# Five copies of half stacks for each head: from engine operations to transfers inside SBUF

## The chip, the core and the metric

The kernel runs on one core of a Trainium2 chip. The metric is the time of one execution on the device, in microseconds; the median of three runs is given. The core has a matrix engine (TensorE, PE in the profile, with its weight loads as PEld), a vector engine (VectorE, DVE), an activation engine (ScalarE, ACT), a general engine (GpSimd, POOL) and SyncE (SP), which here does nothing but issue transfers to 16 DMA engines. Each of the five works through its own list of instructions strictly in order; an instruction waits at the head of its list until what it needs is there.

## The reference

Attention with a mask from hashes, and a two-layer network behind it. q, k and v have 4 batches, 8 heads, 768 positions and 64 features. The six signs of q times `proj` make a bucket number for each position, those of k likewise; a query sees only the keys of its own bucket.

```python
mask = q_bucket[:, :, :, None] == k_bucket[:, :, None, :]
scores = scale * np.matmul(q, k.transpose(0, 1, 3, 2))
scores = np.where(mask, scores, -1000000000.0)
scores = scores - np.max(scores, axis=-1, keepdims=True)
attn = np.exp(scores)
attn = attn / (np.sum(attn, axis=-1, keepdims=True) + 1e-09)
attn_out = np.matmul(attn, v).astype(np.float32)
x = attn_out.transpose(0, 2, 1, 3).reshape(B * S, H * D)   # 3072 tokens, 512 features
h = np.maximum(x @ w_in, 0.0)                               # 512 to 2048
out = (h * h @ w_out).astype(np.float32)                    # 2048 to 512
```

## The kernel before

**Recording and planning.** No instruction is issued where it is written. A recording layer collects every operation with its rank (`pr.rank`), its reads and its writes; some operations are recorded with several ways, the same work as an instruction of one engine or of another. A planner then goes over the recorded list with a price for each instruction (`Program.cost`: a duration for the engine's instructions; for a transfer an issue time and its bytes over a rate), chooses a way for each operation and an order for each engine, and does that in four rounds of passes forward and backward. The result is five lists, which are issued. So a price of one kind of transfer enters the place of every operation of the kernel. Nearly all instructions carry the line of the issuing call (L402; groups of matmuls L399), and tiles tell them apart. Where the plan has TensorE idle ahead of the first `pm`, filler matmuls (`idle`, L395) are put in, in proportion to that idle time.

**The attention.** Work is by pairs of heads. `prep` (L564 to 610) loads a head's R (q transposed in partitions 0 to 63, k transposed in 64 to 127), makes `pd` and `bits` (the hashes), and from them stacks of 128 partitions whose product is q times k plus a term for the buckets. T is partitions 0 to 63 and U is 64 to 127. In batches 1 to 3 (24 heads) numbers are split into a rounded part and a rest for the fast float32r form: A (rounded q and k, on ScalarE), L (the rest, on VectorE), and M (the buckets, on VectorE from `pc`). Then halves are moved between stacks: Q[T] from A[U], Q[U] from L[U], A[U] from A[T], L[U] from M[T], M[T] from Q[T]. So of the five copies two depend on earlier copies directly (M[T] waits for Q[T], A[U] is overwritten only when Q[T] has read it), and L[U] is overwritten only when Q[U] has read it. Each copy moves 64 partitions of 768 float32, 192 KB. A, L, Q and M have two buffers each, one for each head of a pair; a head's stacks are built when the last score matmul of the head two before is done. Batch 0 ("plain") uses float32 matmuls on two stacks and other copies, which stay.

**A unit of scores.** `unit` (L651 to 673) treats 128 queries of one head: four matmuls into `pS` (A by Q, then M by L, in two halves of 384 keys), `nmx` (the row maximum, VectorE), `e` (exponential with row sum, ScalarE), `rv` (reciprocal of the sum), `hl` (probabilities as a float16 part and a float16 rest: ScalarE, then VectorE) and one DMA transpose of hl into aT (384 KB). A head has six units, three for each half of its queries. `av` multiplies aT with the split values VV into `pA` (36 matmuls for a head pair and 384 queries, two side by side in the array), and ScalarE and VectorE make `xx` of it. Four xx feed one pass of `moe`: 16 times 12 matmuls `pm`, the squared and split `g` (ScalarE and VectorE, some on GpSimd), and 9 matmuls `po` for each g. The first pm needs the sixth xx. The weights w_in and w_out come in as float32 `raw` and are split into float16 pairs (`top`, `f`, `win`, `wo`; `sq`, `pt`, `norm` for their scales); that is done ahead of the passes that use them, mostly in the first 150 us.

**What the change touches.** `move` (L429) records a copy with the ways ScalarE, VectorE, GpSimd and, where asked, a transfer; `MV` (L424) allows all four. `send` (L426) records one transfer on SP. The copies are L592 to L594 and L607 to L608, and the planner's price of a transfer is L193.

Of the kernel before, what the change touches and what calls it, by code (L numbers as in the profile page):

```python
# [112 lines left out]
class Program:  # L113
# [59 lines left out]
    @staticmethod  # L173
    def cost(key, name, args, kw):

        size = lambda x: int(np.prod(x.shape[1:]))
        column = {F32: 4 / 2.4, F32R: 0.445}
        if name == "matmuls":

            side = {32: 4, 64: 2}.get(size(args[0][0][1]), 1)  # L180
            t = sum(size(a[2]) * column.get(a[2].dtype, 1 / 2.4) + 7 for a, _ in args) / side
            return t, t
        kinds = [x.rec.kind if isinstance(x, View) else "" for x in args]
        ptr = any(isinstance(x, View) and x.shape[-1] == 1 for x in args[2:3])
        n = max(size(args[0]), size(args[1]) if isinstance(args[1], View) else 0)
        if key == "pe":
            t = max(107, size(args[2]) * column.get(args[2].dtype, 1 / 2.4) + 3)
            return t, t
        if name.startswith("dma"):
            b = int(np.prod(args[0].shape)) * mybir.dt.size(args[0].dtype)  # L190
            inside = name == "dma_start_transpose" or kinds[:2] == ["sb", "sb"]
            busy = 1040 if key == "pool" else (650 if inside else 475) + 50 * (key == "act")
            return busy, b / (292 if name == "dma_start_transpose" else 360)  # L193
        if key == "act":
            t = 93 * (isinstance(kw.get("scale"), View) + isinstance(kw.get("bias"), View)) + (51 if "psum" in kinds[:2] else 93) + n / 1.2 + 93 * ("accum_out" in kw)
        elif key == "pool":
            t = 147 + n * (2.1 if args[0].dtype == F32 or args[0].dtype == F32R else 1.88) if name == "tensor_tensor" else 161 + n / 1.2 + 83 * ptr
        else:
            fast = name in ("tensor_copy", "tensor_scalar") and "psum" not in kinds[:2]
            both = len(args) > 3 and isinstance(args[3], View) and args[3].shape[-1] == 1  # L200
            t = 67 + n / (1.92 if fast else 0.96) + 62 * (ptr and (fast or name == "scalar_tensor_tensor")) + 100 * both
        return t, t
# [212 lines left out]
def lsh_attention_moe(ctx: ExitStack, tc, kq, v, proj2, w_in, w_out, consts, out):  # L415
# [6 lines left out]
    T, U = slice(0, D), slice(D, P)  # L422

    MV = (act, dve, pool, sp)  # L424

    def send(out, x):  # L426
        sp.dma_start(out, x)

    def move(out, x, scale=1.0, engines=(act, dve, pool)):  # L429
        ways = [(q, "tensor_scalar", (out, x, scale, 1.0, ALU.mult, ALU.mult), {}) for q in engines if q not in (act, sp)]  # L430
        if act in engines:
            ways.append((act, "activation", (out, x, AF.Identity if isinstance(scale, View) else AF.Copy), {"scale": scale}))
        if sp in engines:
            ways.append((sp, "dma_start", (out if out.dtype == x.dtype else out.bitcast(x.dtype), x), {}))
        pr.add(*ways)

    def left(out, x, scale, part):
        ways = [(dve, "scalar_tensor_tensor", (out, x, scale, part, ALU.mult, ALU.subtract), {})]
        if not isinstance(scale, View) and scale == 1.0:
            ways.append((pool, "tensor_tensor", (out, x, part, ALU.subtract), {}))  # L440
        pr.add(*ways)

    def sb(shape, dtype, name, bufs=1, tag=None):
        return pr.tile(sbp, "sb", shape, dtype, name, BUFS.get(tag or name, bufs), tag)

    def ps(shape, dtype, name, bufs=1, tag=None):
        return pr.tile(psp, "psum", shape, dtype, name, bufs, tag)
# [111 lines left out]
    f32 = lambda x: x.bitcast(F32)  # L559

    def matmuls(*args, start=True, stop=True):
        pr.add((pe, "matmuls", [(a, {"start": start, "stop": stop}) for a in args], {}))

    def prep(b, hp, plain):  # L564
        r0 = pr.rank
        Rs, Rqs = [], []
        for odd in range(2):
            R = sb([P, S], F32, "Q" if odd else "A") if plain else sb([P, S], F32, "R", 2)
            send(R, kq[b, 2 * hp + odd])
            Rs.append(R)  # L570
            if plain:
                Rq = sb([P, S], F32, "R", 2)[T]
                send(Rq, kq[b, 2 * hp + odd, U])
                Rqs.append(Rq)

        pd = ps([P, 512], F32, "pd", tag="misc")[:, 0:HS]
        matmuls(*[(pd[32 * n : 32 * n + 32], pj, Rs[n // 2][:, n % 2 * HS : (n % 2 + 1) * HS]) for n in range(4)])
        bits = sb([P, HS], BF16, "bits")
        act.activation(bits, pd, AF.Sign, scale=2.0**60, bias=thr)
        out = []  # L580
        for odd, R in enumerate(Rs):
            pr.rank = r0
            if plain:
                M = sb([P, S], F32, "M" if odd else "L")
            else:

                A, L, Q, M = [sb([P, S], F32R, name) for name in "ALQM"]
                move(A, R, cst[:, 2:3])
                left(L, R, cst[:, 2:3], f32(A))
            pr.rank = r0 + STACKS  # L590
            if not plain:
                move(Q[T], f32(A[U]), 1.0, MV)  # L592
                move(Q[U], f32(L[U]), 1.0, MV)
                move(A[U], f32(A[T]), 1.0, MV)  # L594
            for half in range(2):
                w = slice(half * HS, (half + 1) * HS)
                n = 2 * odd + half
                pc = ps([P, 512], F32, "pc", tag="misc")[:, 0:HS]
                pe.matmul(pc, sgn[:, n * P : (n + 1) * P], bits, start=True, stop=True)
                dve.tensor_scalar(M[:, w], pc, cst[:, 0:1], cst[:, 1:2], ALU.subtract, ALU.max)  # L600
            if plain:

                move(R[U], M[T], 1.0, MV)
                move(M[T], Rqs[odd], SC)
                out.append(((M, R),))
            else:
                move(L[U], f32(M[T]), 1.0, MV)  # L607
                move(M[T], f32(Q[T]), 1.0, MV)  # L608
                out.append(((Q, A), (M, L)))
        return out  # L610

# [180 lines left out]
    def ready(b, hp, rank, plain):  # L792

        if (b, hp) not in kept or not alive(x for st in kept[b, hp] for ab in st for x in ab):
            pr.rank = rank
            kept[b, hp] = prep(b, hp, plain)
# [64 lines left out]
```

## Time and profile before

| quantity | value |
|---|---|
| median of 3 runs | 935.48 us (934.19 to 935.99) |
| the profiled execution | 930.39 us |
| its span | 928.3 us |
| TensorE busy | 884.9 us (95%) |
| ScalarE busy | 741.1 us (80%) |
| VectorE busy | 646.0 us (70%) |
| GpSimd busy | 77.4 us (8%) |
| DMA engines, share of the span | 64.4% (main queue) |

A busy share is a mean over stages that differ. Ahead of the first pm TensorE does only scores, pA and filler; in the middle it has scores and pm and po to fill with; at the end pm and po alone. TensorE's ends are modelled, so that a matmul that waits inside the pipeline can be counted as busy; the pitch from one matmul to the next in a stretch without waits tells the work. Waits are put down to the releaser that came last.

### The profile page before, as it was taken

The page shows a single profiled execution, that of the slowest core. Times are in us where ns is not written, and L with a number is a line of the kernel's source. Part 1 is how long each engine was busy: PE and PEld are TensorE (multiplying, and loading weights), DVE is VectorE, ACT ScalarE, POOL GpSimd, SP SyncE. Part 2 cuts the span into 40 slices and gives each one's busy share as a digit, 9 for nine tenths or more (in the row PEclk, how much of TensorE's full clock was granted, in tenths as well). Part 3 has the DMA queues.
Part 4 walks back from the last instruction along what each step waited for, and adds up shares of the span by engine and source line. Part 5 has one row for each costly group of instructions (what it writes and reads, how often), then busy time and mean ns, then how long its engine had stood idle before and what let it go on. Part 6 is the DMA issues. An engine that isn't in the chain of part 4 may idle for free. (4 is left out here: it accounts for less than half of the span.)

```text
span 928.3 us, 14714 instructions
## 1 busy us (share of the span) xinstructions
PE 884.9 (95%) x5334; PEld 480.1 (52%) x5334; DVE 646.0 (70%) x1186; ACT 741.1 (80%) x1269; POOL 77.4 (8%) x140
## 2 busy tenths in 40 slices
PE   7878989999999999799999999999999999999997
PEld 5545555445445555455555555555454555554553
DVE  5998999999898877797877766887767651211111
ACT  5888988998999998999898979997979773533433
POOL 0222233310030000010000000000000000000000
PEclk9999999999999999999999999999999999999999
DMA  7999999947777866796767762974566650300000
GB/s 244 258 252 246 244 221 266 242 102 136 145 170 141 159 132 115 170 199 140 155 120 155 125 118 59 185 161 78 111 113 126 110 96 4 82 1 1 35 1 35
DMA packets 319800, 126.55 MB, mean 136 GB/s; under 512 B 303664, under 2 KB 303792, under 8 KB 319728
## 3 DMA queue, kind: packets, MB, share of 16 engines
q1 hardware_dynamic: 319728, 125.61, 64.4%
q8 instruction: 42, 0.69, 0.3%
q14 instruction: 30, 0.25, 0.1%
HBM read 43.59 MB, written 6.29 MB: 54 GB/s over the span
## 5 line engine op out<-in xcount | busy, mean ns | idle before, releaser
L402 PE MATMUL po<-wo,g 128*128 128x512 f16 x1152 | 332.6, 381 | 1.7 <-ACT o L402 0.9
L402 PE MATMUL pm<-xx,win 128*128 128x384 f16 x1536 | 318.1, 326 | 2.9 <-DVE xx L402 1.7
L402 DVE SCALAR_TENSOR_TENSOR hl<-e,rv,hl 128x768 f16<-128x768 f32 x192 | 195.4, 1020 | 27.0 <-ACT hl L402 25.7
L402 DVE TENSOR_REDUCE nmx<-pS 128x1 f32<-128x768 f32 x192 | 182.8, 952 | 41.4 <-PE pS L402 40.3
L402 PEld LDWEIGHTS <-win 128*128 128x128 f16 x1536 | 145.6, 98 | 119.1 <-issue 21.8
L402 ACT ACTIVATE hl<-e,rv 128x768 f16<-128x768 f32 x187 | 173.6, 930 | 23.6 <-DMA aT<-hl 12.2
L402 ACT ACTIVATE e<-pS,nmx 128x768 f32<-128x768 f32 x192 | 171.0, 891 | 23.6 <-DVE nmx L402 16.3
L402 PEld LDWEIGHTS <-g 128*128 128x128 f16 x1152 | 107.1, 98 | 133.3 <-issue 31.6
L402 DVE SCALAR_TENSOR_TENSOR g<-g,g 128x384 f16<-128x384 f32 x118 | 65.4, 554 | 128.9 <-ACT g L402 128.1
L402 ACT ACTIVATE g<-pm 128x384 f32<-128x384 f32 x127 | 61.5, 484 | 102.0 <-PE pm L402 101.5
L399 PE MATMUL pA<-aT,VV 128*64 128x384 f16 x1152 | 125.9, 333 | 4.1 <-DMA aT<-hl 4.0
L402 ACT ACTIVATE g<-g 128x384 f32<-128x384 f32 (+1 forms) x232 | 120.0, 519 | 4.4 <-PE po L402 0.8
L402 PE MATMUL pS<-A,Q 128*128 128x384 f32 x288 | 92.7, 401 | 6.6 <-ACT e L402 5.7
L399 PEld LDWEIGHTS <-VV 128*64 128x64 f16 x1152 | 58.3, 109 | 68.8 <-issue 48.7
L402 POOL TENSOR_SCALAR rv<-sm 128x1 f32<-128x1 f32 x89 | 33.5, 376 | 564.9 <-ACT e L402 563.9
L402 PE MATMUL pS<-L,M 128*128 128x384 f32 x288 | 77.7, 348 | 0.6 <-ACT M L402 0.6
L402 PEld LDWEIGHTS pS<-A,Q 128*128 128x128 f32 x288 | 46.2, 188 | 45.2 <-ACT e L402 38.4
L402 PEld LDWEIGHTS pS<-L,M 128*128 128x128 f32 x288 | 52.4, 188 | 1.4 <-ACT M L402 0.8
L395 PEld LDWEIGHTS <-ones 128*128 128x128 bf16 x498 | 34.4, 106 | 18.1 <-issue 12.5
L402 PE MATMUL pS<-A,L 128*128 128x384 f32 x96 | 36.6, 504 | 6.9 <-ACT e L402 4.7
L402 PE MATMUL pS<-Q,M 128*128 128x384 f32 x96 | 37.9, 511 | 5.0 <-ACT e L402 3.3
L402 DVE TENSOR_SCALAR M<-pc,cst 128x384 fp32r<-128x384 f32 (+1 forms) x56 | 37.5, 670 | 3.8 <-PE pc L402 3.8
(96 smaller groups left out, 695.8 us busy)
## 6 DMA issues: line engine op xcount, KB each, us to landing
RV<-vp SPq DMA_DIRECT2D x32, 384.0 KB
R<-kq SPq DMA_DIRECT2D x24, 384.0 KB
raw<-w_in SPq DMA_DIRECT2D x16, 511.8 KB
raw<-w_out SPq DMA_DIRECT2D x16, 511.8 KB
out<-o SPq DMA_DIRECT2D x21, 256.0 KB
aT<-hl SPq DMA_TRANSPOSE x192
A<-kq SPq DMA_DIRECT2D x4, 384.0 KB
Q<-kq SPq DMA_DIRECT2D x4, 384.0 KB
```

The source lines that it names most:

```text
L395: issue(q, q.engine.matmul(self.idle[0].real(), self.idle[1].real(), self.idle[1].real(), start=True, stop=True).ins)
L399: ins = q.engine.matmul(*map(real, args), **kw).ins
L402: ins = getattr(q.engine, o.name)(*map(real, o.args), **{k: real(x) for k, x in o.kw.items()}).ins
```

## The change

The five copies of a head in batches 1 to 3 are recorded as transfers on SP alone, no longer as a choice. The planner's rate for a transfer goes from 360 to 314 bytes for each ns, that for a transpose from 292 to 175.

```diff
-            return busy, b / (292 if name == "dma_start_transpose" else 360)
+            return busy, b / (175 if name == "dma_start_transpose" else 314)
...
             if not plain:
-                move(Q[T], f32(A[U]), 1.0, MV)
-                move(Q[U], f32(L[U]), 1.0, MV)
-                move(A[U], f32(A[T]), 1.0, MV)
+                send(f32(Q[T]), f32(A[U]))
+                send(f32(Q[U]), f32(L[U]))
+                send(f32(A[U]), f32(A[T]))
...
             else:
-                move(L[U], f32(M[T]), 1.0, MV)
-                move(M[T], f32(Q[T]), 1.0, MV)
+                send(f32(L[U]), f32(M[T]))
+                send(f32(M[T]), f32(Q[T]))
```

Of the 120 copies the planner had put 117 on ScalarE, 2 on VectorE and 1 on SP; now 120 are on SP. The whole order is made anew. Counts that differ: filler matmuls 498 before and 756 now; `top` on VectorE 3 and 19, on GpSimd 29 and 13; `rv` on GpSimd 89 and 74; runs of pA after the first pm 140 and 115. TensorE's other instructions are the same set in another order.

ScalarE in the middle of the kernel, around the preparation of one head (A<-R begins it; g belongs to moe, e and hl to units). Before:

```order
L402 ACTIVATE A<-R,cst 128x768
L402 ACTIVATE g_5586<-pm 128x384
L402 ACTIVATE Q<-A 64x768
L402 ACTIVATE e,sm<-pS,nmx 128x768
L402 ACTIVATE g_5586<-g_5586 128x384
L402 ACTIVATE Q<-L 64x768
L402 ACTIVATE hl<-e,rv 128x768
L402 ACTIVATE A<-A 64x768
L402 ACTIVATE e,sm<-pS,nmx 128x768
L402 ACTIVATE L<-M 64x768
L402 ACTIVATE hl<-e,rv 128x768
L402 ACTIVATE M<-Q 64x768
```

And in the changed kernel, around a head at a like place:

```order
L402 ACTIVATE A<-R,cst 128x768
L402 ACTIVATE hl<-e,rv 128x768
L402 ACTIVATE e,sm<-pS,nmx 128x768
L402 ACTIVATE g_6387<-pm 128x384
L402 ACTIVATE hl<-e,rv 128x768
L402 ACTIVATE g_6387<-g_6387 128x384
L402 ACTIVATE g<-g_6387 128x384
L402 ACTIVATE e,sm<-pS,nmx 128x768
L402 ACTIVATE hl<-e,rv 128x768
L402 ACTIVATE g_6446<-pm 128x384
```

The five copies between A<-R and the next head's work are gone from ScalarE; e, hl and g close up.

SP's list, the only one of transfers. Before, where the one copy stands that was a transfer (RV and R are loads, aT the transposes):

```order
L402 DMA_TRANSPOSE aT<-hl 128x12x128
L402 DMA RV<-vp 128x768
L402 DMA_TRANSPOSE aT<-hl 128x12x128
L402 DMA A<-A 64x768
L402 DMA R<-kq 128x768
L402 DMA_TRANSPOSE aT<-hl 128x12x128 x5
```

And in the changed kernel, around one head in the middle:

```order
L402 DMA Q<-A 64x768
L402 DMA Q<-L 64x768
L402 DMA R<-kq 128x768
L402 DMA_TRANSPOSE aT<-hl 128x12x128
L402 DMA L<-M 64x768
L402 DMA A<-A 64x768
L402 DMA_TRANSPOSE aT<-hl 128x12x128
L402 DMA M<-Q 64x768
```

Five transfers of each head now stand between the transposes, in the order in which SP issues them.

VectorE just ahead of the sixth xx, which releases the first pm. Before, where 236 operations stand ahead of that xx:

```order
L402 RECIPROCAL rv<-rv 128x1
L402 SCALAR_TENSOR_TENSOR win<-f,towin,win 128x512
L402 TENSOR_SCALAR fromwo<-norm 128x1
L402 RECIPROCAL rv<-rv 128x1
L402 TENSOR_REDUCE rows<-RV 128x12
L402 SCALAR_TENSOR_TENSOR f<-raw,top_77 128x512
L402 SCALAR_TENSOR_TENSOR xx<-pA,xx 128x384
```

And in the changed kernel, where 291 stand ahead of it:

```order
L402 SCALAR_TENSOR_TENSOR win<-f,towin,win 128x512 x2
L402 TENSOR_REDUCE nmx<-pS 128x1
L402 SCALAR_TENSOR_TENSOR hl<-e,rv,hl 128x768
L402 SCALAR_TENSOR_TENSOR f<-raw,top_73 128x512
L402 TENSOR_SCALAR top_77<-raw 128x512
L402 RECIPROCAL rv<-rv 128x1
L402 SCALAR_TENSOR_TENSOR xx<-pA,xx 128x384
```

The weights' splitting (top, f, win, wo) and a few units of scores moved ahead of it: 14 more top, 4 more each of f, win and wo, 3 more each of hl and nmx, 10 more rv, 7 more back and some smaller ones. On TensorE 6 more float32 score operations of batch 0 and 7 more pt stand ahead of the first pm.

## Rows read from the trace of the kernel before

**Rows 1.** The page: its span, and each engine's busy time and share.

```profile
span 928.3 us, 14714 instructions
PE 884.9 (95%) x5334; PEld 480.1 (52%) x5334; DVE 646.0 (70%) x1186; ACT 741.1 (80%) x1269; POOL 77.4 (8%) x140
```

**Rows 2.** The chain, pieces without a wait: start us, us, engine, tile, line, count.

```profile
918.68 4.11 PE po L402 x19
...
905.27 1.14 PE pm L402 x7
...
490.40 2.07 PE pA L399 x24
...
489.09 0.70 PE pS L402 x4
```

**Rows 3.** Groups of TensorE's instructions: count, busy us, mean ns, idle before.

```profile
L402 PE MATMUL po<-wo,g 128*128 128x512 f16 x1152 | 332.6, 381 | 1.7 <-ACT o L402 0.9 <-ACT wo L402 0.7
L402 PE MATMUL pm<-xx,win 128*128 128x384 f16 x1536 | 318.1, 326 | 2.9 <-DVE xx L402 1.7 <-ACT g L402 1.0
L399 PE MATMUL pA<-aT,VV 128*64 128x384 f16 x1152 | 125.9, 333 | 4.1 <-DMA aT<-hl 4.0
```

**Rows 4.** TensorE in order of time: start us, us; the first pm.

```profile
148.81 0.33 PE L402 MATMUL pm<-xx,win 128*128 128x384 f16 x1
```

**Rows 5.** Busy time by stretch; its first line names the columns.

```profile
core 0: us, PE busy (x) PEld busy (x) DVE busy (x) ACT busy (x) POOL busy (x), PEclk, DMA share, GB/s
50.00:150.00 100.00, 87.04 (x624) 50.83 (x623) 93.37 (x167) 86.58 (x144) 27.13 (x44) 0.98 1.11 242
200.00:450.00 250.00, 240.60 (x1444) 130.87 (x1444) 210.66 (x385) 236.29 (x400) 19.43 (x37) 1.00 0.73 148
450.00:750.00 300.00, 296.95 (x1758) 160.11 (x1755) 222.75 (x400) 260.86 (x445) 8.01 (x21) 1.00 0.65 123
750.00:850.00 100.00, 99.56 (x554) 51.40 (x552) 23.63 (x42) 44.07 (x87) 0.00 (x0) 1.00 0.14 31
```

**Rows 6.** Waits from 150 to 750 us: us in total, times, longest us.

```profile
PEld pS L402 <- ACT e L402: 40.1, 90, 2.3
```

**Rows 7.** One of the five groups of copies: count, busy us, mean ns.

```profile
L402 ACT ACTIVATE Q<-A 64x768 fp32r<-64x768 f32 x24 | 20.2, 843 | 0.6
```

**Rows 8.** ScalarE in order of time, around one head's copies.

```profile
460.51 0.84 ACT L402 ACTIVATE Q<-A 64x768 fp32r<-64x768 f32 x1
461.38 0.90 ACT L402 ACTIVATE e<-pS,nmx 128x768 f32<-128x768 f32 x1
...
466.57 0.84 ACT L402 ACTIVATE L<-M 64x768 fp32r<-64x768 f32 x1
467.44 0.93 ACT L402 ACTIVATE hl<-e,rv 128x768 f16<-128x768 f32 x1
468.28 0.83 ACT L402 ACTIVATE M<-Q 64x768 fp32r<-64x768 f32 x1
469.02 0.88 ACT L402 ACTIVATE e<-pS,nmx 128x768 f32<-128x768 f32 x1
```

**Rows 9.** SP's issues in order of time: the one copy that was a transfer.

```profile
245.80 0.52 SPq L402 DMA_DIRECT2D A<-A  x1
```

**Rows 10.** Two short stretches behind that issue; columns as in rows 5.

```profile
245.80:246.90 1.10, 1.10 (x9) 0.50 (x9) 1.10 (x2) 1.07 (x2) 0.00 (x0) 1.00 0.00 0
246.90:248.40 1.50, 1.41 (x9) 0.63 (x7) 1.03 (x2) 1.47 (x2) 0.00 (x0) 1.00 1.00 195
```

**Rows 11.** The chain around 694 us: a transpose that is waited for.

```profile
693.81 4.41 DMA aT<-hl
```

**Rows 12.** VectorE in order of time: the second half of that head's M.

```profile
465.80 0.68 DVE L402 TENSOR_SCALAR M<-pc,cst 128x384 fp32r<-128x384 f32 x1
```

**Rows 13.** TensorE in order of time: score matmuls after that head's copies.

```profile
470.50 0.70 PE L402 MATMUL pS<-A,Q 128*128 128x384 f32 x2
474.08 0.64 PE L402 MATMUL pS<-A,Q 128*128 128x384 f32 x2
```

**Rows 14.** Groups of VectorE's instructions from 0 to 149 us; columns as in rows 3.

```profile
L402 DVE SCALAR_TENSOR_TENSOR hl<-e,rv,hl 128x768 f16<-128x768 f32 x38 | 38.7, 1018 | 1.9 <-ACT hl L402 1.7
L402 DVE SCALAR_TENSOR_TENSOR win<-f,towin,win 128x512 f16<-128x512 f32 x12 | 9.2, 775 | 0.0
L402 DVE TENSOR_SCALAR top<-raw 128x512 f16<-128x512 bf16 x2 | 1.0, 478 | 0.3 <-DMA raw<-w_in 0.3
```

## The prediction, made before the changed kernel ran

> **What bounds the kernel now.** I read the page's busy shares first. In the profiled execution the span is 928.3 us and TensorE is busy for 95% of it [rows 1]; the run took 930.39 us, and the median of the three timed runs is 935.48, which is 1.0055 times that. A busy matmul can be one that waits inside the pipeline, so the second view is the chain of waits with its pitches, taken where TensorE waits for nothing: 19 po in 4.11 us (0.216 each), 7 pm in 1.14 (0.163), 24 pA in 2.07 (0.081 each, with about 0.11 us to change into the group's tiling), 4 pS of float32r in 0.70 (0.175) [rows 2]. With the counts [rows 3] I ask how much of the time after the first pm is work. That pm starts at 148.81 us [rows 4]: everything ahead of it is attention, the weights' splitting and filler. After it come 1152 po (248.8 us), 1536 pm (250.4), 936 of the 1152 pA (the sixth xx needs 216 first; 75.8), 24 x 24 = 576 float32r score matmuls (100.8), 140 changes into and out of the pA tiling at about 0.21 (29.4) and, an estimate from their counts, some 30 us of hash, norm and first-batch score matmuls: 735. The last po ends at 918.68 + 4.11 = 922.8, so 774 us pass and **about 39 are lost**; 5.5 follow for the output. The kernel's time is therefore three numbers: the start of the first pm, the work left then, and the loss.
>
> The windows tell where the loss lies. TensorE is idle for 9.4 of 250 us from 200 to 450, where ScalarE is busy for 236.3 (95%); for 3.1 of 300 from 450 to 750 with ScalarE at 87%; for 0.4 of 100 from 750 to 850 with it at 44% [rows 5]. And the waits name the releaser: in the middle of the kernel the loads of score matmuls wait 40.1 us for `e` on ScalarE, in 90 places, far more than for anything else (loads overlap matmuls, so this is no sum of lost time) [rows 6]. ScalarE's queue is what starves TensorE in the middle; ahead of the first pm it is VectorE, busy for 93.4 of 100 us from 50 to 150 [rows 5].
>
> **What leaves ScalarE.** A head of batches 1 to 3 has five copies: 24 heads, 120 copies, 117 of them on ScalarE in five groups like the one shown, 2 on VectorE, 1 a transfer already. One lasts 0.843 us [rows 7]. ScalarE runs without a gap around a head: Q<-A at 460.51 and the next at 461.38, 0.87 apart; L<-M 466.57 and the next at 467.44, 0.87; M<-Q 468.28 with the next at 469.02, 0.74, because this one overlaps its successor [rows 8]. A head costs 4 x 0.87 + 0.74 = 4.2 us, so ScalarE loses some 98 us of work. Ten heads are prepared between 200 and 450: 236.3 - 42 = 194 of 250 (78%); twelve between 450 and 750: 260.9 - 50 = 211 of 300 (70%).
>
> What is that worth? I divide the 39 us: about 34 between 150 and 750, in proportion to the idle time: 21.6 in 200 to 450 (8.6% of it), 7.0 in 450 to 750 (2.3%), 5.4 in 150 to 200. The curve of loss against ScalarE's share is steep: 0.4% at 44%, 2.3% at 87%, 8.6% at 95%. On the curve, 78% gives 1.9% and 70% gives 1.6%, together 9.5 us where 28.6 were: a gain of 19. On a straight line through the ends it would be 9. Nothing excludes 0 (a chain pS, nmx, e, pS that waits for its own length and not for a queue). The three points bend, so I take **-17**, bounds 0 and -28.
>
> **What SP and the DMA engines get.** 119 more transfers of 192 KB stand in SP's one queue, between the transposes; an SP issue takes 0.5 us and engines no longer do the copies, so the issue itself costs no engine anything but SP. The transfer's length decides. The one case in the trace is issued at 245.80 [rows 9]; up to 246.90 the DMA engines carry nothing, then they run at share 1.00 and 195 GB/s, with a load of R behind it [rows 10]. So a copy lands no sooner than about 1.1 + 1.0 = 2.1 us after its issue. The far end is the transpose of an hl, of twice the bytes, whose piece in the chain is 4.41 us [rows 11]. I take 2.7, nearer to the first, because that row is the same operation. The copies form a chain for a head: after mask M is complete, L[U]<-M[T] and then M[T]<-Q[T]. M is ready near 466.5 (it starts at 465.80), M<-Q ends at 469.11 [rows 8, 12], and pS follow at 470.50 and 474.08 [rows 13]; the rows don't tell which of them is the new head's first, so the slack is 1.4 or 5.0. Two transfers of 2.7 end at 471.9: 2.8 us later than now, which is inside one slack and outside the other. The plan is made anew with the copies as transfers, and can prepare a head sooner; I put this at **0** in the sum, bounds 0 and +24 (1 us a head).
>
> The Trainium skill (SBUF — State Buffer, The DMA setup-cost knee and Door 1: The DMA port swizzle) speaks against the change: each DMA pays a roughly fixed 2 us, and 64 partitions reach only half of the ports, about 218 GB/s. By it a copy is an estimated 2.9 us, two of them end at 472.3, and where half the heads have the short slack the sum moves by 12 x 0.4 = 5 us for the worse. The trace shows less than the fixed part before the first packet (1.1 us) and has no landing of a lone copy, so it neither bears the 2.9 out nor refutes it.
>
> **What moves ahead of the first pm.** Because two prices of the planner changed, all of the order is new. TensorE's real instructions are the same set, but ahead of the first pm there is more of everything, and filler rises from 498 to 756. Most of all VectorE: the sixth xx, on which the first pm waits, stood behind 236 operations and now behind 291. Added are 14 top (0.478 each, 6.7 us: from GpSimd, whose share of them falls), 4 win (0.775), 4 wo and 4 f of about the same size (9.1 together), 3 hl (1.018) and 3 nmx (5.9 together) [rows 14], and about 25 small ones (some 4): 26 us, less 0.1 for each overlap, **22**. With VectorE full there, the first pm comes later by nearly that: **+20**, to about 169; bounds +12 (the 7% in which VectorE idles, and waits for raw that go) and +24. TensorE's order then also has more done by then: 6 float32 score operations of two matmuls (at 0.35, 4.2 us), 7 pt (1.5) and 25 fewer pA groups in what follows (140 to 115, 25 x 0.21 = 5.3): **-11** of work after it.
>
> The sum: 20 - 11 - 17 = **-8**. Span 920, run 922.4, median 922.4 x 1.0055 = **927**. Extremes of the terms give -27 and +13 without a late copy.
>
> **Rivals.** *Late copies (slower).* The DMA engines are at share 0.73 from 200 to 450 [rows 5]; a copy takes them for 1.0 us, 50 copies for 50 us there, +0.20: 0.93. If copies then queue behind transposes, one takes 4.4 or more, two end near 475.5, 6.4 us later than now, past both slacks by 1.4 to 5. SP's queue has its own share in it: a copy that waits for its M holds up every transpose and load behind it, and pA waits for these. At 1 us a head, 24 heads are +24 on the forecast: +16, median about 951. It decides from 0.33 us a head (8 / 24). For: the share, the thin slack. Against: today's transposes already overlap with little harm, and ScalarE's 10 us from A to M<-Q are now free of its queue. *The start is late and the loss stays.* If scores wait for the length of their own chain, the copies on ScalarE were a filling of its gaps: +20 - 11 - 0 = +9, median 944. For: hl of ScalarE is moved there and VectorE stays as full. Against: ScalarE has no gap around a head [rows 8]. *Nothing that can be measured.* Half of the gain on the loss: within 2 us of 935. The change does do what it says: 119 of the 120 copies stand in SP's order.
>
> **Chances.** The forecast (with its own range 914 to 933) 0.58, late copies 0.20, the late start alone 0.10, nothing 0.12. A difference under 0.2%, 1.9 us, can't be told from none. Faster 0.60, same 0.14, slower 0.26. To leave out 2 in 10: low 914 (-21), high 944, which holds the late start and the lesser half of the late copies.
>
> **What would show it.** First pm between 161 and 173 us; ScalarE's busy time near 741 - 98 = 643; its waits of scores for `e` halved; TensorE idle from 200 to 450 under 6 us. A copy's landing under 3.5 us; no pS that waits for M or L. It is wrong where pS waits for a DMA into L or M, where the first pm is beyond 175, or where the idle time stays at 9 in that stretch with ScalarE under 80%.

## The result, and the profile after

The changed kernel takes 923.17 us (median of 4 runs, 922.39 to 925.36), the kernel before 935.74 in the same comparison: a ratio of 0.9878, with a 95% interval of 0.9852 to 0.9904. It is 12 us faster, where 8.5 were forecast; 927 was the predicted time, 914 to 944 the range.

Here is the page of the changed kernel: span and engines, then its main DMA queue (packets, MB, share of 16 engines), to be held against [rows 1].

```profile
span 923.6 us, 15264 instructions
...
PE 885.6 (96%) x5592; PEld 501.3 (54%) x5592; DVE 643.8 (70%) x1206; ACT 663.6 (72%) x1166; POOL 54.8 (6%) x104
...
q1 hardware_dynamic: 329248, 149.02, 73.6%
```

ScalarE is relieved of 77.5 us. The profiled executions differ by less than the medians: spans 928.3 and 923.6, runs 930.39 and 925.36. That of before is shorter than all of its 4 timed runs, that of after the longest of its 4, so the traces show 5 of the 12 us in their place. The granted clock is part of the rest: its mean over a run is 0.998 in the median of the changed kernel's four runs (0.996 in the one traced) and 0.994 or 0.995 for the kernel before in the later comparisons (0.997 in the one traced). What 0.004 of the clock costs is at most 0.004 x 930 = 3.7 us by an estimate from these figures; that is not all of the 7 us.

Busy time by stretch, columns as in [rows 5]:

```profile
50.00:150.00 100.00, 88.07 (x742) 55.09 (x738) 95.20 (x187) 81.39 (x136) 17.48 (x29) 1.00 1.01 228
200.00:450.00 250.00, 242.97 (x1473) 137.82 (x1471) 206.75 (x385) 205.31 (x354) 20.77 (x38) 0.99 0.94 202
450.00:750.00 300.00, 299.58 (x1823) 167.96 (x1821) 223.76 (x403) 229.82 (x413) 5.09 (x13) 1.00 0.79 165
```

TensorE's idle time falls from 9.4 to 7.0 us in the second line and from 3.1 to 0.4 in the third; ScalarE from 95 to 82% and from 87 to 77%; the DMA engines go up from 0.73 to 0.94 and from 0.65 to 0.79. The waits from 150 to 750 us, to be held against [rows 6]:

```profile
PEld pS L402 <- ACT e L402: 21.3, 42, 2.1
...
PE pS L402 <- ACT e L402: 8.4, 13, 1.7
...
PEld pS L402 <- DMA M<-Q: 0.7, 2, 0.6
```

and, of the kernel before, the matmuls' own wait:

```profile
PE pS L402 <- ACT e L402: 6.1, 19, 0.7
```

The loads that waited for `e` wait half as long (40.1 to 21.3); the matmuls themselves wait 2.3 us more. For the copies almost nobody waits. And TensorE in order of time at its first pm, which was at 148.81 [rows 4]:

```profile
167.89 1.56 PE L402 MATMUL pS<-A,L 128*128 128x384 f32 x4 [0.74 <-ACT e L402]
169.28 0.38 PE L402 MATMUL pt<-sq,ones 128*128 128x512 bf16 x1
169.50 1.30 PE L402 MATMUL pm<-xx,win 128*128 128x384 f16 x7
```

**The sum of the prediction, for every kernel.** The prediction splits the time into the start of the first pm, the work left then (counts times the pitches of [rows 2]) and the loss. The same count was made in the trace of each kernel that ran. The loss is the remainder, and the work left holds the prediction's estimate of some 30 us in every row, so rows can be compared but no row proves the split. "Ratio" is to the kernel before, as it ran beside that kernel. One run of experiment 9 (950.40 us, granted clock 0.94) fell in a slower state and is left out of its row.

| kernel | median us | ratio, 95% interval | first pm | last po ends | work left | loss |
|---|---|---|---|---|---|---|
| before | 935 | 1 | 148.8 | 922.8 | 736 | 38 |
| changed | 923.2 | 0.9878 (0.9852 to 0.9904) | 169.5 | 918.4 | 725 | 24 |
| 1: changed order, copies on ScalarE | 987.7 | 1.0557 (1.0534 to 1.0581) | 169.6 | 980.5 | 725 | 86 |
| 2: order of before, copies on SP | 1002.7 | 1.0710 (1.0688 to 1.0732) | 152.8 | 994.7 | 736 | 106 |
| 3: new prices only | 932.1 | 0.9966 (0.9950 to 0.9983) | 156.0 | 925.1 | 732 | 37 |
| 4: transfers only | 949.7 | 1.0154 (1.0123 to 1.0185) | 153.3 | 945.9 | 729 | 63 |
| 5: changed, a twin for each copy | 991.4 | 1.0599 (1.0546 to 1.0651) | 170.2 | 986.2 | 725 | 91 |
| 6: changed, top on GpSimd | 925.8 | 0.9898 (0.9868 to 0.9928) | 168.7 | 919.3 | 725 | 26 |
| 7: transfers, one new price | 935.5 | 1.0010 (0.9991 to 1.0028) | 159.0 | 926.0 | 728 | 39 |
| 8: three of five as transfers | 917.1 | 0.9812 (0.9767 to 0.9857) | 158.3 | 909.3 | 725 | 26 |
| 9: before, hl and aT shifted | 937.1 | 1.0023 (1.0006 to 1.0041) | 155.9 | 932.8 | 736 | 41 |
| 10: changed, hl and aT shifted | 927.8 | 0.9918 (0.9897 to 0.9939) | 169.1 | 920.6 | 725 | 27 |
| 11: as 4, hl and aT shifted | 938.0 | 1.0033 (1.0010 to 1.0057) | 155.2 | 927.5 | 729 | 43 |
| 12: as 7, hl and aT shifted | 926.9 | 0.9916 (0.9894 to 0.9939) | 158.6 | 918.7 | 728 | 32 |

### The profile page after: what moved, and what is told of

It is laid out like the page before. It is cut to its first block, busy times and chain, and to the rows that moved or that the text cites. A ratio compares the mean times of both kernels' runs of the same rounds, so it can differ in the third digit from the quotient of the medians.

```text
span 923.6 us, 15264 instructions
## 1 busy us (share of the span) xinstructions
PE 885.6 (96%) x5592; PEld 501.3 (54%) x5592; DVE 643.8 (70%) x1206; ACT 663.6 (72%) x1166; POOL 54.8 (6%) x104
## 4 chain that ended last, share of the span: by engine, by line
PE 63%; ACT 5%; DMA 2%; DVE 2%; issue 1%; POOL 0%; SPq 0%; ACTq 0%; DVEq 0%
PE po L402 23%; PE pm L402 21%; PE pS L402 9%; PE pA L399 8%; ACT wo L402 1%; DMA aT<-hl 1%; ACT e L402 1%; PE pd L399 1%; DMA RV<-vp 1%; ACT hl L402 1%; DVE hl L402 1%; ACT g L402 1%; PE pc L402 1%; DVE nmx L402 1%; DMA M<-Q 1%
## 5 line engine op out<-in xcount | busy, mean ns | idle before, releaser
L402 PE MATMUL pm<-xx,win 128*128 128x384 f16 x1536 | 322.4, 327 | 1.3 <-DVE g L402 1.0
L402 DVE SCALAR_TENSOR_TENSOR g<-g,g 128x384 f16<-128x384 f32 x122 | 67.5, 554 | 127.7 <-ACT g L402 127.1
L402 ACT ACTIVATE g<-g 128x384 f32<-128x384 f32 (+1 forms) x248 | 128.8, 520 | 10.8 <-PE po L402 5.6
L399 PE MATMUL pA<-aT,VV 128*64 128x384 f16 x1152 | 117.8, 331 | 0.0
L402 PE MATMUL pS<-A,Q 128*128 128x384 f32 x288 | 95.2, 411 | 5.0 <-ACT e L402 4.8
L402 PEld LDWEIGHTS pS<-A,Q 128*128 128x128 f32 x288 | 49.3, 190 | 29.8 <-ACT e L402 15.9
L402 POOL TENSOR_SCALAR rv<-sm 128x1 f32<-128x1 f32 x74 | 28.8, 389 | 610.6 <-ACT e L402 604.0
L395 PEld LDWEIGHTS <-ones 128*128 128x128 bf16 x756 | 49.9, 103 | 20.1 <-issue 11.8
L395 PE MATMUL idle<-ones 128*128 128x128 bf16 x756 | 54.7, 228 | 2.7 <-DVE ones L402 2.7
```

What stands on the lines that cost most here:

```text
L395: issue(q, q.engine.matmul(self.idle[0].real(), self.idle[1].real(), self.idle[1].real(), start=True, stop=True).ins)
L399: ins = q.engine.matmul(*map(real, args), **kw).ins
L402: ins = getattr(q.engine, o.name)(*map(real, o.args), **{k: real(x) for k, x in o.kw.items()}).ins
```

## The experiments

The planner makes a new order from any edit, so a comparison of two edits compares two orders as well. For eight of the twelve experiments the order was therefore held: the planner works as in one kernel, and only at the issue of its lists is something exchanged. The theories: (1) relief of ScalarE is the gain; (2) the new prices are, and who copies is worth nothing; (3) a copy as a transfer is late and costs. Theories P, Q and R are named in experiments 9 and 11; A and B are, each time, those of the experiment's own expectation.

**1. The changed order, the copies on ScalarE.**

```diff
-            ins = getattr(q.engine, o.name)(*map(real, o.args), ...).ins
+            q, name, args, kw = o.swap or (q, o.name, o.args, o.kw)   # the copies: act, "activation", Copy
+            ins = getattr(q.engine, name)(*map(real, args), ...).ins
```

> The order of every engine is that of the changed kernel; only the five copies of a head are issued on ScalarE, at the place in the order where the changed kernel issues their transfers. Theory 1 (the transfers relieve ScalarE, and that is the gain): the first pm stays near 169 us, ScalarE is busy about 98 us more, waits for e come back, and the time is 10 to 20 us above the changed kernel: 933 to 943. Theory 2 (the gain is the new order, made with prices nearer to the chip; who carries the copies is worth nothing): 921 to 926. Theory 3 (a copy as a transfer is late, and costs): below 921.

987.65 us, 6.9% above the changed kernel by the ratios (1.0557 / 0.9878). The first pm does not move; the loss goes from 24 to 86. The waits of scores from 150 to 750:

```profile
PEld pS L404 <- ACT e L404: 64.9, 72, 3.2
...
PE pS L404 <- ACT e L404: 38.1, 48, 2.1
```

Theory 1 has the direction, but more than three times the size: this order sets 98 us of work on ScalarE where it left no place for it. It is the opposite of theory 2's claim that the carrier is worth nothing, but no measure of what the relief is worth to an order made for ScalarE.

**2. The order of before, the copies on SP.** The exchange of experiment 1 the other way round, in the kernel before.

```diff
-                move(Q[T], f32(A[U]), 1.0, MV)
+                movesp(Q[T], f32(A[U]))   # planned as move(..., MV); issued as sp.dma_start; so all five
```

> The order of every engine is that of the kernel before; only the copies leave ScalarE and VectorE and are issued as transfers on SP at their place in the order. Theory 1: the first pm stays near 149 us, ScalarE loses 98 us of work, the loss behind the first pm falls by up to 17 us less what late copies take back (an order that allowed 0.9 us for a copy now gets some 2.7 to 3.8): 918 to 933. Theory 2: 933 to 938. Theory 3 (late copies decide where the order has no room for them): above 940, with score matmuls that wait for a DMA into L or M.

1002.66 us, the slowest of all. Theory 3 holds here, and theory 1 fails as a statement on the carrier alone. What the copies cost is seen in the waits from 150 to 750 us, and in the chain around 468 us:

```profile
PE pS L404 <- DMA M<-Q: 43.5, 18, 6.4
...
PEld pS L404 <- DMA M<-Q: 9.1, 3, 4.3
```

```profile
464.58 3.52 DMA L<-M
468.10 0.02 issue
468.12 3.01 DMA M<-Q
471.12 0.14 issue
471.26 0.59 PE pS L404 x2
```

The pair behind M is serial: L[U]<-M[T] lands 3.5 us after its issue, only then is M[T]<-Q[T] issued, and score matmuls start when it lands. 6.5 us here, where ScalarE did the two within 2.5 [rows 8]. This is the rival "late copies" with its mechanism and its place. Part of the cost is the clock that went with the waits:

```profile
200.00:450.00 250.00, 223.35 (x1304) 121.50 (x1303) 190.93 (x353) 179.72 (x312) 20.83 (x37) 0.96 0.84 172
450.00:750.00 300.00, 269.37 (x1535) 144.97 (x1533) 199.11 (x362) 192.25 (x346) 9.41 (x18) 0.94 0.76 151
```

TensorE is idle for 27 and 31 us of these stretches, and the granted clock is 0.96 and 0.94 where it was 1.00 [rows 5]. By an estimate from these rows that is up to 0.04 x 250 + 0.06 x 300 = 28 of the 68 us by which the loss grew.

**3. New prices only.**

```diff
-            return busy, b / (292 if name == "dma_start_transpose" else 360)
+            return busy, b / (175 if name == "dma_start_transpose" else 314)
```

> Only the planner's two rates change (314 and 175 bytes per ns); the five copies keep their choice, and ScalarE keeps nearly all of them. Theory 1: the late start comes from the rates (filler 678 against 498 and 756), the middle stays as full as before: 930 to 940. Theory 2: most of the gain, 922 to 928.

932.05 us, 0.3% faster. As theory 1 has it, the loss stays at 37, and ScalarE in the middle is as full as before:

```profile
200.00:450.00 250.00, 238.88 (x1452) 133.67 (x1453) 213.29 (x398) 237.51 (x395) 19.88 (x36) 0.99 0.66 152
```

The changed kernel has the same prices, so the step from here to it is what the copies as transfers are worth with them: 0.9% by the ratios (0.9966 and 0.9878), with a loss of 24 instead of 37 and a start that is 13.5 us later.

One number did not fit: the share of the DMA engines is 0.66 here and 0.73 in the same stretch of the kernel before, with no fewer bytes. Experiments 9 to 12 come from it.

**4. Transfers only.** The five `send` of the change, the rates left at 360 and 292.

> Only the five copies become transfers; the planner's rates stay at 360 and 292. Theory 1: ScalarE is relieved as in the changed kernel and the start stays early (filler 510 against 498): the first pm near 150 us, the loss near 25, 912 to 922, better than the changed kernel unless the order made with the old rates has transposes that come too late. Theory 2: 930 to 937. Theory 3: above 935.

949.66 us: 1.5% slower, against theory 1. ScalarE is relieved (195 of 250 us from 200 to 450), and the loss still grows from 38 to 63:

```profile
PEld pS L402 <- ACT e L402: 29.5, 42, 4.1
...
PE pS L402 <- ACT e L402: 14.5, 16, 3.4
PE pS L402 <- DMA M<-Q: 14.0, 11, 3.3
...
PEld pS L402 <- DMA M<-Q: 9.4, 8, 3.6
```

So each half of the change is worth little or costs, and both together gain 1.2%. Copies are late in this order. Not all of that is the old prices: experiment 11 gives 12 of the 15 us to the place of two tiles.

**5. A twin for each copy.** In the changed order, a second transfer of the same bytes from the same source into DRAM.

```diff
             issue(q, ins)
+            if o.twin:
+                issue(q, q.engine.dma_start(o.twin, real(o.args[1])).ins)
```

> The order of the changed kernel; behind each of the 120 copies SP issues a second transfer of the same 192 KB, from the same source to a scratch place in DRAM that nobody reads. This doubles what the copies cost SP's queue (120 x 0.5 us) and the DMA engines (120 x about 1 us, share 0.94 to about 1.15 from 200 to 450 us), and nothing else. Theory A (the order leaves room for the copies and the DMA engines have some left): 923 to 929. Theory B (the copies land just in time and any further queueing makes score matmuls wait for M<-Q): 935 to 960, with copies landing in 4 us or more and pS that wait for a DMA.

991.42 us, 7% above the changed kernel; theory B, beyond its upper end.

```profile
PEld pS L403 <- ACT e L403: 36.7, 55, 3.3
PE pS L403 <- DMA M<-Q: 26.9, 11, 4.2
PEld pS L403 <- DMA M<-Q: 24.5, 10, 4.4
```

The changed kernel works at the edge: SP's queue and the DMA engines have no room for another such load. Which of the two is the narrower this run does not tell, as it burdens both. Here too the clock is lower (0.95; 0.99 in the changed kernel):

```profile
200.00:450.00 250.00, 222.17 (x1277) 122.58 (x1276) 180.95 (x338) 179.98 (x309) 19.13 (x35) 0.95 0.99 210
```

**6. top on GpSimd.** In the changed order, the 19 `top` of VectorE are issued on GpSimd.

```diff
+            if o.to and q.key == "dve":
+                q = o.to
```

> The order of the changed kernel; only the 19 top that VectorE has are issued on GpSimd at their place. Theory A (VectorE, full ahead of the first pm, sets its start): 16 of them stand ahead of it, 16 x 0.48 = 7.7 us, so the first pm comes at 162 to 165 and the time is 916 to 920. Theory B (the start is set by the loads of raw or by the chain raw, top, f, which gets longer by 0.94 - 0.48 us for each): the first pm stays at 168 to 172, and the time at 921 to 928.

925.75 us; the changed kernel's own ratio, 0.9878, lies within the interval of this one. The first pm, in TensorE's order of time:

```profile
167.05 1.56 PE L405 MATMUL pS<-A,L 128*128 128x384 f32 x4 [0.74 <-ACT e L405]
168.44 0.38 PE L405 MATMUL pt<-sq,ones 128*128 128x512 bf16 x1
168.66 1.30 PE L405 MATMUL pm<-xx,win 128*128 128x384 f16 x7
```

It is 0.8 us earlier where theory A wanted 7. 16 operations of 0.45 us taken from VectorE's list change next to nothing, so the length of that list alone does not set the start. The run is no clean test of VectorE, though. Up to 170 us `f` on VectorE now waits for `top` on GpSimd, where one takes 0.92 us:

```profile
DVE f L405 <- POOL top L405: 3.6, 5, 1.9
```

And what stands right ahead of the pm in TensorE's own list is a float32 score matmul that waits for `e`, in both kernels; that `e` waits for a `nmx` on VectorE, first in the changed kernel and then here:

```profile
166.84 0.90 ACT L402 ACTIVATE e<-pS,nmx 128x768 f32<-128x768 f32 x1 [2.71 <-DVE nmx L402]
166.01 0.90 ACT L405 ACTIVATE e<-pS,nmx 128x768 f32<-128x768 f32 x1 [2.71 <-DVE nmx L405]
```

So VectorE is one part of a chain that goes through TensorE, ScalarE and VectorE. Whether that chain of scores of batch 0 sets the start was not tried.

**7. Transfers, and the new price of a transpose alone.**

```diff
-            return busy, b / (292 if name == "dma_start_transpose" else 360)
+            return busy, b / (175 if name == "dma_start_transpose" else 360)
```

> The five copies are transfers and the price of a transpose is the new one (175), but a plain transfer keeps its old price (360). Theory A (what makes the transfers pay is the dearer transpose, since a copy queues behind transposes and the order then leaves room for that): 920 to 928, pS waits for M<-Q under 3 us in all. Theory B (the copies' own price matters as much: 0.55 us of data at 360, 0.63 at 314): 930 to 945.

935.53 us, no difference from before: theory B as far as it goes, and a riddle, for 0.08 us in the price of a copy should not decide 12 us. Score matmuls do wait for copies (10.6 us and, in the loads, 9.8). Most of the answer is in experiment 12.

**8. Three of the five as transfers.** New prices; the two copies behind M stay operations.

```diff
-                send(f32(L[U]), f32(M[T]))
-                send(f32(M[T]), f32(Q[T]))
+                move(L[U], f32(M[T]), 1.0, (act, dve, pool))
+                move(M[T], f32(Q[T]), 1.0, (act, dve, pool))
```

> New prices; three copies of a head are transfers (Q from A, Q from L, A from A), the two behind the mask M stay operations of an engine. ScalarE is relieved of 72 x 0.87 = 63 us and not of 98. Theory A (ScalarE's relief is the gain, and in the changed kernel the copies behind M cost nothing any more): 925 to 931, between the kernel with new prices only (932) and the changed one (923). Theory B (the two serial copies behind M still take back part of the gain): 916 to 922.

917.13 us: theory B's figure, and the best of all kernels, 0.7% below the changed one by the ratios, whose intervals just touch. The table does not bear out theory B's reason, though. The loss is 26, no less than with five transfers; what is better is the start, 158.3 instead of 169.5. The stretches:

```profile
200.00:450.00 250.00, 242.47 (x1497) 137.94 (x1496) 215.22 (x399) 225.69 (x390) 22.05 (x37) 1.00 0.85 186
450.00:750.00 300.00, 298.61 (x1807) 167.81 (x1806) 218.86 (x393) 242.30 (x431) 11.82 (x19) 1.00 0.68 147
```

ScalarE at 90% loses as little here as at 82% in the changed kernel, and with the new prices alone, at 95%, the loss was 37: over these three orders the first few per cent of relief bring all of it. The orders differ in more than that, the DMA engines among it (0.85 here, 0.94 in the changed kernel), so this is a reading and no proof. Why this order starts sooner is not known.

**9. Before, with hl and aT 32 bytes further.** The trace's semaphore events give, for each transpose, the time from SP's issue to its last part. The shortest of a kernel was 3.17 us in the changed kernel and in experiments 1, 3, 5, 6 and 8, and 3.63 to 3.65 in the kernel before and in 2, 4 and 7. The built programs differ by the same line in the place of the transposes' tiles: in the first group hl begins at byte 80128 of each partition and aT at 89600, both multiples of 256; in the second at 80096 and 89312, both 32 bytes short of one. Tiles get their place when they are first used, and a new order puts small tiles (ident, top, dg) ahead of hl or behind. (raw and bits lie elsewhere by the same line; experiments 9 to 12 leave them where they are.) Theory P: this place is a part of the gain. Theory Q: it is none. (The expectations speak of multiples of 64, which holds too; no run tells 64 from 256.)

```diff
+            if name == "hl" and "pad" not in self.pads:
+                self.pads["pad"] = pool.tile([P, 8], F32, name="pad", tag="pad", bufs=1)
...
+            if name == "aT" and "pad2" not in self.pads:
+                self.pads["pad2"] = pool.tile([P, 8], F32, name="pad2", tag="pad2", bufs=1)
```

The second tile stands behind aT. So the tiles that come after (VV, win, wo, xx, g and small ones) move by 64 bytes as well, while the stacks of the copies stay in their places. The length of a transpose is tested by this; for the kernel's time the places of those other tiles are a rival that no run takes apart.

> The kernel before with the same order; only hl and aT lie 32 bytes further in SBUF, at multiples of 64 bytes, as they happen to lie in the changed kernel (a new order of first uses places small tiles otherwise). Seen so far: the shortest landing of a transpose is 3.17 us where hl and aT lie so (the changed kernel, e1, e3, e5, e6, e8) and 3.63 to 3.67 where they lie 32 bytes off (before, e2, e4, e7). Theory P (the place decides the transposes' length): shortest landing 3.17, DMA share from 200 to 450 us about 0.66 instead of 0.73, and since TensorE seldom waits for a transpose here, 930 to 934. Theory Q (the order and the prices make the difference, the place does nothing): landing 3.63, time 934 to 936.

The shortest transpose takes 3.17 us now, and the packets of the same bytes take less of the 16 engines. The queue in the kernel before, and here:

```profile
q1 hardware_dynamic: 319728, 125.61, 64.4%
```

```profile
q1 hardware_dynamic: 319728, 125.61, 59.1%
```

Theory P is right on the transposes. But the time is 937.08, 0.2% above the kernel before, not below. That the DMA engines had room to spare without the copies (0.73 [rows 5]) is a reading that fits; this run can't show it, as its clock was lower as well (0.991 in the median run, 0.994 for the kernel before beside it). Its trace shows where it was longer than that of before:

```profile
50.00:150.00 100.00, 82.43 (x577) 47.11 (x573) 86.47 (x153) 82.15 (x137) 21.94 (x41) 0.95 1.06 228
```

The granted clock is 0.95 in this stretch (a mean of its two levels, 2.4 and 1.2 GHz, with a tenth of the time at the lower), against 0.98 in the kernel before [rows 5], and the first pm comes at 155.91, 7 us later in the same order. The profiled run took 940.36, among the longer ones. TensorE has gaps in that stretch; the changed kernel, with 756 filler matmuls and not 498, has a clock of 1.00 there. That the changed kernel's steadier start is where its runs keep the higher clock is a guess that fits; it was not tested.

**10. The changed kernel, with hl and aT 32 bytes further.** The same edit; hl and aT now lie 32 bytes past the multiples of 256.

> The changed kernel with the same order; hl and aT lie 32 bytes further, off the multiples of 64 bytes, as in the kernel before. Theory P: shortest landing of a transpose 3.63 us, the DMA engines (share 0.94 from 200 to 450 us) have no room for that, copies land later, score matmuls wait for M<-Q by 10 to 25 us in all: 930 to 945; a good part of the change's gain then hangs on the place. Theory Q: 922 to 925.

927.81 us, 0.4% above the changed kernel: 0.9918 (0.9897 to 0.9939) against 0.9878. Theory P by its direction, but less than it wanted. The shortest transpose takes 3.65 us, and:

```profile
PEld pS L409 <- DMA M<-Q: 4.1, 5, 1.3
PE pS L409 <- DMA M<-Q: 3.9, 6, 1.7
```

These are the waits for a copy that were 0.7 us. About 4 of the change's 12 us hang on where hl and aT happened to lie; most does not. The two intervals overlap by a little, so 4 us is a rough size, though no run of this kernel was as short as the longest of the changed one (925.56 and 925.36).

**11. Transfers only, with hl and aT at multiples of 256.**

> The kernel with transfers and the old prices (949.7 us), same order, hl and aT at multiples of 64 bytes. Theory P alone (the place explains why that kernel was slow): 920 to 930. Theory R (place and prices each have a share, since the old prices leave less room for a copy): 935 to 943. Theory Q: 946 to 952.

937.97 us, where 949.66 was: 12 us from 32 bytes. Theory R fits: place and prices each have a share. The waits for a copy fall, and so do those for `e`:

```profile
PEld pS L409 <- ACT e L409: 23.6, 35, 1.8
PE pS L409 <- ACT e L409: 9.9, 14, 1.3
PE pS L409 <- DMA M<-Q: 9.4, 9, 3.4
PEld pS L409 <- DMA M<-Q: 6.4, 5, 3.6
```

**12. Transfers and one new price, with hl and aT at multiples of 256.**

> The kernel with transfers, the new price of a transpose and the old one of a plain transfer (935.5 us), same order, hl and aT at multiples of 64 bytes. Theory P: 922 to 928, so that the price of a plain transfer (360 or 314) mattered only through the place that its order gave to hl. Theory R: 929 to 933. Theory Q: 934 to 937.

926.87 us, where 935.53 was, and 0.9916 against the changed kernel's 0.9878. Most of the riddle of experiment 7 was the place: the price of a plain transfer gave an order in which hl fell 32 bytes elsewhere. With the place right, its own worth is 0.4% or less (the intervals overlap); the price of a transpose is worth 1.2% (938 against 927, experiments 11 and 12). The waits:

```profile
PEld pS L409 <- ACT e L409: 13.4, 33, 1.9
PEld pS L409 <- DMA M<-Q: 6.6, 6, 3.6
...
PE pS L409 <- DMA M<-Q: 5.1, 3, 3.1
PE pS L409 <- ACT e L409: 5.0, 8, 1.7
```

Against experiment 11 those for a copy fall only from 15.8 to 11.7 us, those for `e` from 33.5 to 18.4. How the price of a transpose brings its gain is therefore not shown; room for the copies is at most a part of it.

**The four corners.** Four kernels have hl and aT at multiples of 256 and differ in copies and prices. With the old prices the copies on ScalarE give 1.0023 (experiment 9) and the transfers 1.0033 (11); with the new prices they give 0.9966 (3) and 0.9878 (changed). The transfers are worth nothing that can be told with the old prices, and 0.9% with the new ones; the prices are worth 0.6% without the transfers. This is the plainest statement of the gain: it needs both.

## Why the prediction was right, and where it was not

*The frame.* Start, work left and loss: forecast +20, -11, -17; in the two traces +20.7, -10.9 and -14. The sum of -8 came out as -4.4 for the last po, and the start was found within 1 us of 169. As the loss is what remains, the frame itself can't fail; what was forecast are its terms.

*The step to the median, and luck.* The traced run was forecast at 922.4 and took 925.36, 3 us more, because the loss fell by less. The median was forecast at 1.0055 times the traced run, as in the kernel before, and was 0.9976 times it. So 927 was too high by 4 us where the sum was too low by 3: the nearness of the forecast is in part two errors of opposite sign.

*ScalarE.* The copies left it, and the loads' waits for `e` halved (40.1 to 21.3). The busy time fell by 77.5 us and not 98: the new order also gives it work, 16 more g of 0.52 us among it. In the steep curve of loss against ScalarE's share the form was right and the knee was wrong. By the prediction's reading, a share of 82% should lose some 2%; experiment 8 has 90%, and its loss is within 2 us of the changed kernel's. In these orders all of the gain lies between 95 and 90%; no run moved ScalarE's share with the rest held.

*The start.* Its time was right and its reason is not borne out. The prediction sized it by VectorE's list, 22 us longer; experiment 6 takes 7 us out of that list, and the start moves by 0.8, though part of the 7 may have come back as waits for GpSimd. The likeness of 22 and 20.7 may be chance, or both follow from the same order. What sets it stays open.

*The copies.* The term was put at 0 with a bound of +24, on the ground that the plan is made anew with the copies as transfers. In the changed kernel it is 0.7 us of waits. But the prediction did not see on what this rests. A copy takes, from issue to last part, 2.5 us at the least and 2.8 (the two into Q) to 3.8 (A<-A) in the median; 2.7 was the size of an undisturbed one. The prediction says that the trace has no landing of a lone copy; by the semaphore events it has one, 2.73 us after the issue at 245.80. In an order that was not made for it a copy is late and costs 7% (experiment 2); with the old prices it costs (4) or takes back what it gives (11): the rival was no remote case, with a chance of 0.20, but what happens unless the order leaves room. That the price of the transposes is worth 1.2% with the transfers (experiments 11 and 12) was not in the prediction at all; the change's two lines of prices were read only as the cause of a new order.

The estimate of 2.9 us from the Trainium skill (SBUF — State Buffer, The DMA setup-cost knee and Door 1: The DMA port swizzle) is nearer than 2.7 to three of the five medians (3.1 to 3.8 us) and no nearer to the two into Q (2.8), while the shortest copies, 2.5 us, lie below it. Its warning, that a small transfer pays mostly a fixed time, no run here tests, as no run changes the size of a copy; what two of them cost in a row is the 6.5 us of experiment 2.

*The margin on the DMA engines.* The share of 0.93 in the middle was forecast, 0.94 came, and it was right to call that thin: experiment 5 loses 7% to one more transfer for each copy.

*What had no part in it.* The place of hl and aT. The change moved them by chance from 32 bytes short of a multiple of 256 onto one, and that is worth some 0.4% of the 1.2 (experiment 10).

## What to carry to other kernels

Work that is taken from a full engine and given to a queue changes its length as well as its place: 0.84 us on ScalarE became 2.5 to 3.8, and the gain was there only where the order had been made for that. So give the planner the price together with the transfer: neither alone brought more than a part. Try the serial steps on the engine too: the three copies ahead of M as transfers and the two serial ones behind it on an engine were better than all five by 0.7%, though by an earlier start and not by fewer late copies. And when a new order comes out faster or slower than its parts explain, look where its tiles lie before explaining it.

## What the runs showed of the hardware

In these kernels a DMA transpose of 384 KB of float16 from [128 x 1536] takes 3.17 us at the least from issue to last part when source and target start at multiples of 256 bytes in each partition, and 3.63 to 3.65 when they start 32 bytes off; in the kernel before that is 64.4 against 59.1% of the DMA engines' time for the same bytes (experiment 9). The Trainium skill (DMA: Bandwidth & Descriptors, How a descriptor splits into AXI transactions) says that a transaction starts at a 256-byte boundary and that a descriptor which doesn't start there fetches bytes it does not use; the longer transposes 32 bytes off agree with it, though these runs moved source and target together and can't say which of them pays.

A score matmul can wait in TensorE's list behind nothing but a 192 KB copy for up to 6.4 us (experiment 2), twice the 3.01 us of that run's M<-Q at 468 us, when two such copies are serial.
